# Cross attention with a maxout layer on one core: the first batch's casts and products in another order and on other engines

## The chip, the cores and the metric

The kernel runs on one core of one Trainium2 chip. A core has five engines with a queue each, which work their instructions off in order and wait for one another by semaphores: TensorE (PE in the profile; PEld is its loading of weights), VectorE (DVE), ScalarE (ACT), GpSimd (POOL) and SyncE (SP), which here issues nearly all transfers. The metric is the device time in microseconds (us) of one execution; it is compared by the median of several.

## The reference

There are 8 batches of 8 heads. In each, 512 rows of `x` attend to 32 rows of `state` and the other way round, with 64 elements per row. Both results, joined, are the input of a layer with two weights and a maximum, and an output weight.

```python
a = softmax(scale * x @ state.T);   xread = a @ state       # per batch and head
a2 = softmax(scale * state @ x.T);  sread = a2 @ x
t = concatenate([xread, sread])     # rows of all heads: (4352, 512)
h1 = t @ w1; h2 = t @ w2            # 512 x 1024 each
out = maximum(h1, h2) @ w_out       # 1024 x 512, result in float32
```

## The kernel before

**Algebra.** max(h1, h2) is relu(h1 − h2) + h2. So the kernel forms WD = W1 − W2 (`wd`) and W2Wo = W2 @ Wo (`wwo`), and since xread is a @ state it also forms state @ WD and state @ W2Wo per batch (the tiles `sw`, functions `sw_mm` and `sw_ev`). Per batch, the first layer is then relu(a · (state·WD)) (`l1_mm`, `l1_ev`, tile `r`), and the output is r @ Wo + a · (state·W2Wo) (`l2_part`, `l2_open`, tile `acc`). All matmuls are in bfloat16; the inputs arrive in float32 and are cast.

**Stages.** From batch 2 on the work is a steady loop. Batch 0, and the preparation of the weights beside it, is written out call by call in lines 604 to 877, and the order of these lines is the order on every engine's queue (a manual schedule; waits are added where data or a buffer require them). The change lies there, in lines 668 to 745.

**Loads.** SP's queue loads `x` of batch 0, then the first quarter (256 columns) of W2, W1 and Wo in two halves of 128 columns, then the other three quarters, then batches 1 to 3. W1, W2 and Wo have three float32 buffers each (`w1f`, `w2f`, `wof`), so the fourth quarter of W2 (line 623) waits until the first quarter's buffer has been read for the last time, which is the subtraction `w_sub(0, ...)`.

**Attention of batch 0.** Heads go in four pairs, k = 0 to 3. For each pair the exponentials `e` are summed over 32 states, the sums of two pairs are inverted together (`norm_sums`), and `e` is multiplied by the inverses into `a`: for pairs 0 and 1 together by `norm_mul(0, 0, "P")` on GpSimd (128x512 elements), for pair 3 by `norm_mul_pair` on VectorE (128x256), and for pair 2 in two halves of 128 elements, one on GpSimd and one on VectorE. `at_mm` transposes `a` on TensorE and `at_ev` copies it out of PSUM (tile `aT`); `l1_mm` needs both copies.

**Weights of the first quarter**, by halves j of 128 columns: `w2_cast_h`, `w1_cast_h`, `wo_cast_h` cast them; `sw_h_mm(j)` forms state·W1 − state·W2 from the casts, without waiting for `wd`; `w2_tr_h_mm` and `w2_tr_h_ev` transpose W2; `w_wo_h_mm(i, j)` is one W2Wo matmul for row block i and half j, `w_wo_ev(0, i)` copies the sum of both halves into the float32 tile `w2acc`. Later quarters do it with `w2_cast`, `w_sub`, `w2_tr_mm`, `w_wo_mm(r, i)` and `sw_two_mm`.

**PSUM** has two pools of four banks, `ps` and `pa`; a call's pool argument chooses. The tiles `acc` of batch 0 hold four banks of `pa` from `l2_part` on. **`idle(n)`** issues n matmuls of a zero tile with 256 columns, which compute nothing that is used.

An engine is named by a letter in the calls: "P" GpSimd, "V" VectorE, "A" ScalarE. All copies and casts go through one helper, so their lines in the profile are 58 (ScalarE), 60 (VectorE) and 62 (GpSimd).

Of the kernel before, what the change touches and what calls it, by code (L numbers as in the profile page):

```python
# [15 lines left out]
def kernel(  # L16
# [11 lines left out]
    _, _, Ns, _ = state.shape  # L28
# [3 lines left out]
    NC = S // 128  # L32
# [14 lines left out]
    pa = ctx.enter_context(tc.tile_pool(name="pa", bufs=4, space=bass.MemoryType.PSUM))  # L47
    ctx.enter_context(tc.manual_schedule())

    def bank(dtype=F32, pool=None):  # L50
        n = 512 if dtype == F32 else 1024
        if pool is pa:
            return pa.tile([128, n], dtype, tag="acc", name="acc")
        return ps.tile([128, n], dtype, tag="ps", name="ps")

    def copy(eng, o, i):
        if eng == "A":
            nc.scalar.copy(o, i)  # L58
        elif eng == "V":
            nc.vector.tensor_copy(o, i)  # L60
        else:
            nc.gpsimd.tensor_copy(o, i)  # L62
# [74 lines left out]
    P = {}  # L137
# [5 lines left out]
    def state_mm(b, pool=None):  # L143
        p = P["st", b] = bank(BF16, pool)
        nc.tensor.transpose(p[:, 0:128], sb0[:, b], ident)
# [69 lines left out]
    def xt_pair_ev(b, k, eng):  # L215
        copy(eng, st[b]["xt"][:, :, k, :], P["xt", k][:, 0:512].rearrange("p (c t) -> p c t", c=NC))
# [79 lines left out]
    def norm_sums(b, hh, sums=True):  # L296
        d = st[b]
        if sums:
            ev = d["e"].rearrange("p g c i n -> p (g c) i n")[:, :, 2 * hh:2 * hh + 2, :]
            nc.vector.tensor_reduce(d["es"][:, hh], ev, axis=mybir.AxisListType.X, op=ALU.add)  # L300
        nc.vector.reciprocal(d["er"][:, hh], d["es"][:, hh])

    def norm_mul(b, hh, eng):
        d = st[b]
        ev = d["e"].rearrange("p g c i n -> p (g c) i n")[:, :, 2 * hh:2 * hh + 2, :]
        av = d["a"].rearrange("p g c i n -> p (g c) i n")[:, :, 2 * hh:2 * hh + 2, :]
        (nc.gpsimd if eng == "P" else nc.vector).tensor_mul(  # L307
            av, ev, d["er"][:, hh].unsqueeze(3).to_broadcast([128, 2 * NC, 2, Ns]))

    def norm_mul_pair(b, k, eng, g0=0, g1=2):  # L310
        d = st[b]
        gs = slice(NC * g0, NC * g1)
        ev = d["e"].rearrange("p g c i n -> p (g c) i n")[:, gs, k, :]
        av = d["a"].rearrange("p g c i n -> p (g c) i n")[:, gs, k, :]
        (nc.gpsimd if eng == "P" else nc.vector).tensor_mul(
            av, ev, d["er"][:, k // 2, gs, k % 2].unsqueeze(2).to_broadcast([128, NC * (g1 - g0), Ns]))

    def norm(b, hh, eng, sums=True):
        norm_sums(b, hh, sums)
# [13 lines left out]
    def at_mm(b, g, pool=None):  # L333
        if b not in AT:
            AT[b] = keep.tile([128, 2, NC, 128], BF16, tag="at", name="aT")
        p = P["at", g] = bank(BF16, pool)
        for c in range(NC):
            nc.tensor.transpose(p[:, c * 128:(c + 1) * 128], st[b]["a"][:, g, c].rearrange("p i n -> p (i n)"), ident)

    def at_ev(b, g, eng):  # L340
        copy(eng, AT[b][:, g].rearrange("p c t -> p (c t)"), P["at", g][:, 0:512])
# [12 lines left out]
    def sread_norm(b):  # L354
        d = st[b]
        sr = d["sr"] = at.tile([128, 2, D], BF16, tag="sr", name="sr")
        rr = at.tile([128, 2], F32, tag="rr", name="rr")
        pv = d["srp"][:, 0:130].rearrange("p (g d) -> p g d", g=2)
        for g in range(2):
            nc.vector.reciprocal(rr[:, g:g + 1], pv[:, g, 64 * g:64 * g + 1])  # L360
        for g in range(2):
            nc.vector.tensor_scalar(sr[:, g, :], pv[:, g, 1 - g:65 - g], scalar1=rr[:, g:g + 1], scalar2=None,
                                    op0=ALU.mult)
# [21 lines left out]
    def sw_ev(b, lo, hi, g, eng):  # L385
        copy(eng, SW[b][:, g, lo:hi], P["sw", b, lo][g][:, 0:hi - lo])
# [28 lines left out]
    def sw_h_mm(j, pool):  # L415

        cs = slice(128 * j, 128 * j + 128)
        pg = P["sw", 0, 128 * j] = [bank(F32, pool), bank(F32, pool)]
        for t, w in ((sbd[:, 0], w1b), (sbdn, w2b[0])):
            for i in range(4):  # L420
                for g in range(2):
                    nc.tensor.matmul(pg[g][32 * i:32 * i + 32, 0:128], t[64 * g:64 * g + 64, i, 32 * g:32 * g + 32],
                                     w[64 * g:64 * g + 64, i, cs], start=(w is w1b), stop=(w is not w1b))
# [18 lines left out]
    def l1_mm(b, f, pool=None):  # L442
        if b not in R:
            R[b] = big.tile([128, NF, NC * 128], BF16, tag="r", name="r")
        p = P["l1", f] = bank(F32, pool)
        for g in range(2):
            nc.tensor.matmul(p, SW[b][:, g, f * 128:(f + 1) * 128], AT[b][:, g].rearrange("p c t -> p (c t)"),  # L447
                             start=(g == 0), stop=(g == 1))
# [71 lines left out]
    def w2_cast(q, eng):  # L520
        w2b[q] = stage.tile([128, 4, FQ], BF16, tag="w2b", bufs=2, name="w2b")
        for j, e in enumerate(eng):
            m = 4 // len(eng)
            copy(e, w2b[q][:, m * j:m * j + m].rearrange("p i f -> p (i f)"),
                 w2f[q][:, m * j:m * j + m].rearrange("p i f -> p (i f)"))

    def w2_cast_h(j, eng):
        if 0 not in w2b:
            w2b[0] = stage.tile([128, 4, FQ], BF16, tag="w2b", bufs=2, name="w2b")
        copy(eng, w2b[0][:, :, 128 * j:128 * j + 128], w2f[0][:, :, 128 * j:128 * j + 128])  # L530

    def w1_cast_h(j, eng):
        copy(eng, w1b[:, :, 128 * j:128 * j + 128], w1f[0][:, :, 128 * j:128 * j + 128])

    def wo_cast_h(j, eng):
        copy(eng, wo[:, j, :], wof[0][:, j, :])

    def w2_tr_h_mm(j, pool=None):
        p = P["w2h", j] = bank(BF16, pool)
        for i in range(4):  # L540
            nc.tensor.transpose(p[:, i * 128:(i + 1) * 128], w2b[0][:, i, j * 128:(j + 1) * 128], ident)

    def w2_tr_h_ev(j, eng):
        copy(eng, w2t[:, j].rearrange("p i t -> p (i t)"), P["w2h", j][:, 0:512])
# [15 lines left out]
    def w_sub(q, i0, i1, eng):  # L560
        (nc.gpsimd if eng == "P" else nc.vector).tensor_sub(  # L561
            wd[:, i0:i1, q * FQ:(q + 1) * FQ], w1f[q][:, i0:i1], w2f[q][:, i0:i1])
# [15 lines left out]
    def w_wo_h_mm(i, j, pool=None):  # L578
        if j == 0:
            P["wwo", 0, i] = bank(F32, pool)  # L580
        nc.tensor.matmul(P["wwo", 0, i], w2t[:, j, i, :], wo[:, j, :], start=(j == 0), stop=(j == 1))

    def w_wo_ev(r, i, eng):
        if r == 0:
            copy(eng, w2acc[:, i, :], P["wwo", r, i])
        else:
            nc.vector.tensor_tensor(wwo[:, i, :] if r == len(ROUNDS) - 1 else w2acc[:, i, :], P["wwo", r, i],  # L587
                                    w2acc[:, i, :], op=ALU.add)
# [3 lines left out]
    def idle(n, cols=256):  # L592
        if idle_p[0] is None:
            idle_p[0] = bank(F32, pa)
        for j in range(n):
            nc.tensor.matmul(idle_p[0][:, 0:cols], wz[:, 0:128], wz[:, 0:cols], start=True, stop=True)  # L596
# [71 lines left out]
    xt_pair_mm(0, 3)  # L668
    norm_sums(0, 0, False)
    norm_mul(0, 0, "P")  # L670
    xt_pair_ev(0, 3, "A")
    idle(1)
    scores_pair_mm(0, 2, None)
# [10 lines left out]
    sw_h_mm(0, pa)  # L684
    reduce_pair(0, 3)
    norm_sums(0, 1, False)
    norm_mul_pair(0, 2, "P", 0, 1)
    norm_mul_pair(0, 3, "V")
    norm_mul_pair(0, 2, "V", 1, 2)
    wo_cast_h(0, "P")  # L690
    w1_cast_h(1, "P")
    w2_tr_h_ev(0, "A")
    sw_ev(0, 0, 128, 1, "A")
    idle(4)
    at_mm(0, 0)
    sw_ev(0, 0, 128, 0, "A")
    at_mm(0, 1)
    w_wo_h_mm(1, 0, pa)
    wo_cast_h(1, "P")
    w_sub(0, 0, 4, "P")  # L700
    w_wo_h_mm(3, 0)
    w2_cast_h(1, "A")
    at_ev(0, 1, "V")
    sw_h_mm(1, pa)
    sw_ev(0, 128, 256, 1, "V")
    w2_tr_h_mm(1)
    at_ev(0, 0, "A")
    l1_mm(0, 0)
    sw_ev(0, 128, 256, 0, "A")
    l1_mm(0, 1, pa)  # L710
    w_wo_h_mm(0, 0, pa)
    w2_tr_h_ev(1, "A")
    l1_ev(0, 1, "A")
    copy("A", sb0[:, 1], sf0[:, 1])
# [1 line left out]
    l1_ev(0, 0, "V")  # L716
    w_wo_h_mm(3, 1)
    w_wo_ev(0, 3, "A")
    w2_cast(1, "P")
    w_wo_h_mm(0, 1)  # L720
    w_wo_h_mm(1, 1)
    w_wo_h_mm(2, 1)
    state_mm(1)
    sread_norm(0)
    state_ev(1, "V")
    l2_part(0, 3)
    sw_mm(1, 0, FQ)
    w_wo_ev(0, 1, "A")
    sw_ev(1, 0, FQ, 1, "A")
    l2_part(0, 1)  # L730
    sw_ev(1, 0, FQ, 0, "A")
# [6 lines left out]
    wo_cast_part(1, 1, "P")  # L738
    sw_two_mm(1)
    sw_two_ev(1, 1, "V")  # L740
    w_wo_ev(0, 0, "A")
    l2_part(0, 2)
    w_wo_mm(1, 1)
    w_wo_ev(1, 1, "V")
    w_wo_ev(0, 2, "A")
    w_wo_mm(1, 2)
    sw_two_ev(1, 0, "A")
    l1_mm(0, 3)
# [131 lines left out]
    for b in range(1, B):  # L880
        n = b + 1
# [68 lines left out]
```

## Time and profile before

| | |
|---|---|
| median of 6 executions | 147.06 us (146.8 to 147.61) |
| the profiled execution | 147.61 us, span on the core 145.8 us |
| TensorE busy | 139.2 us, 95% of the span |
| VectorE, ScalarE, GpSimd busy | 85.4, 70.3, 59.4 us |
| transfers | 29.44 MB, 202 GB/s on average, 320 to 364 GB/s from 3.6 to 33 us |

In a row of the timeline the first number is the start in us from the beginning of the span, the second how long the operation or the merged group took; then come engine, line, operation, what it writes and reads, shape and count, and in brackets the engine's idle time before it with what ended it. A row of the chain has start, length and what the time went to. Rows of merged instructions overlap a little, as the next one starts while the last is ending.

### The profile page before, as it was taken

How to read it: one execution, taken by the hardware profiler on the slowest of the kernel's cores; microseconds unless marked ns; L12 is line 12 of the kernel's file. 1: busy time of each engine (PE TensorE's matmuls, PEld its weight loads, DVE VectorE, ACT ScalarE, POOL GpSimd, SP SyncE). 2: the span in 40 equal slices, each digit the busy share in tenths (PEclk: the TensorE clock that was granted, in tenths of full speed). 3: DMA queues.
4: the chain of work that ended last, by engine and by line, in shares of the span. 5: the costliest groups of instructions: out<-in, count | busy, mean ns of one | idle time of the engine just before them, and what ended most of it. 6: DMA issues, size and time to landing. Idle time of an engine off the chain costs nothing.

```text
span 145.8 us, 3202 instructions
## 1 busy us (share of the span) xinstructions
PE 139.2 (95%) x1281; PEld 69.8 (48%) x1300; DVE 85.4 (59%) x176; ACT 70.3 (48%) x136; POOL 59.4 (41%) x82
## 2 busy tenths in 40 slices
PE   6899999999999999999999999999999999999990
PEld 4465444464554445444544544454445344754460
DVE  3595776879788648464854675376557464621110
ACT  4478757786694456326450825271537145511010
POOL 2379633858938431925290547226500500000000
PEclk9999999999999999999999999999999999999999
DMA  5999999999979999388948784887406032402423
GB/s 119 322 321 349 356 362 364 361 349 201 108 153 357 149 321 274 74 195 329 246 52 280 288 180 86 278 295 141 72 18 272 7 72 108 180 4 72 144 101 115
DMA packets 37727, 29.44 MB, mean 202 GB/s; under 512 B 21328, under 2 KB 34896, under 8 KB 36816
## 3 DMA queue, kind: packets, MB, share of 16 engines
q1 hardware_dynamic: 37440, 29.17, 71.4%
q8 instruction: 10, 0.16, 0.5%
q10 hardware_dynamic: 272, 0.07, 0.2%
q14 instruction: 5, 0.04, 0.1%
HBM read 15.34 MB, written 8.91 MB: 166 GB/s over the span
## 4 chain that ended last, share of the span: by engine, by line
PE 77%; DMA 9%; SPq 6%; POOL 3%; DVE 2%; issue 1%; ACT 0%; POOLq 0%
PE acc L463 35%; PE ps L447 16%; PE acc L459 7%; DMA wof<-in_moe_w_out_dram 5%; DMA xt<-xb 4%; PE ps L576 3%; PE ps L503 2%; PE acc L513 2%; PE ps L382 2%; PE ps L284 2%; SPq L130 2%; PE acc L349 1%; SPq L134 1%; SPq L91 1%; PE acc L487 1%
## 5 line engine op out<-in xcount | busy, mean ns | idle before, releaser
L463 PE MATMUL acc<-wo,r 128*128 128x512 bf16 x246 | 59.3, 379 | 0.4
L463 PEld LDWEIGHTS <-r 128*128 128x128 bf16 x248 | 23.8, 98 | 28.7 <-issue 0.6
L58 ACT COPY ob<-acc 128x512 f32<-128x512 f32 (+2 forms) x17 | 9.4, 554 | 48.1 <-PE acc L463 26.7
L447 PE MATMUL ps<-aT,sw 128*128 128x512 bf16 x117 | 27.7, 379 | 0.0
L438 DVE TENSOR_SCALAR r<-ps 128x512 bf16<-128x512 f32 x26 | 18.0, 691 | 14.3 <-PE ps L447 14.2
L307 POOL TENSOR_TENSOR a<-e,er 128x512 bf16<-128x512 bf16 x14 | 14.4, 1049 | 25.8 <-ACT e L289 18.9
L436 ACT ACTIVATE r<-ps 128x512 bf16<-128x512 f32 x33 | 19.6, 602 | 5.5 <-PE ps L447 4.9
L60 DVE COPY ob<-acc 128x512 f32<-128x512 f32 (+1 forms) x17 | 10.9, 646 | 16.3 <-PE acc L463 14.6
L62 POOL CAST xb<-xf 128x1024 bf16<-128x1024 f32 x12 | 12.9, 1082 | 16.4 <-DMA xf<-in_x_dram 16.4
L62 POOL CAST xo<-xf 128x512 bf16<-128x512 f32 x28 | 16.4, 623 | 5.8 <-DMA xf<-in_x_dram 5.4
L447 PEld LDWEIGHTS <-sw 128*128 128x128 bf16 x128 | 12.2, 98 | 13.7
L459 PE MATMUL acc<-sw,aT 128*128 128x512 bf16 x49 | 15.5, 381 | 0.3
L60 DVE CAST sw<-ps 128x512 bf16<-128x512 f32 x15 | 9.8, 686 | 9.9 <-PE ps L382 9.5
L58 ACT CAST sw<-ps 128x512 bf16<-128x512 f32 (+1 forms) x21 | 11.0, 573 | 3.0 <-PE ps L408 1.5
L300 DVE TENSOR_REDUCE es<-e 128x16 f32<-128x512 bf16 x14 | 9.2, 656 | 1.7 <-ACT e L289 1.7
L289 ACT ACTIVATE e<-ps 128x512 bf16<-128x512 f32 x14 | 7.7, 596 | 0.8 <-PE ps L284 0.2
L596 PE MATMUL acc<-wz 128*128 128x256 bf16 x32 | 6.7, 345 | 1.2 <-DVE ones L636 1.2
L459 PEld LDWEIGHTS <-aT 128*128 128x128 bf16 x62 | 5.0, 98 | 4.4
L576 PE MATMUL ps<-wo,w2t 128*128 128x512 bf16 x23 | 6.6, 379 | 0.2
L587 DVE TENSOR_TENSOR w2acc<-ps,w2acc 128x512 f32<-128x512 f32 x8 | 5.1, 684 | 1.2 <-PE ps L576 1.2
L561 POOL TENSOR_TENSOR wd<-w1f,w2f 128x1024 bf16<-128x1024 f32 x2 | 4.7, 2365 | 1.7 <-DMA w1f<-in_moe_w_dram 1.7
L284 PEld LDWEIGHTS <-xt 128*128 128x128 bf16 x112 | 4.3, 98 | 1.9 <-DMA xt<-xb 0.2
(109 smaller groups left out, 146.4 us busy)
## 6 DMA issues: line engine op xcount, KB each, us to landing
xf<-in_x_dram SPq DMA_DIRECT2D x14, 512.0 KB, 5.6
out_dram<-ob SPq DMA_DIRECT2D x7, 1024.0 KB, 4.2
w2f<-in_moe_w_dram SPq DMA_DIRECT2D x3, 512.0 KB, 7.4
xf<-in_x_dram SPq DMA_DIRECT2D x4, 256.0 KB, 3.9
w1f<-in_moe_w_dram SPq DMA_DIRECT2D x4, 256.0 KB, 6.6
wof<-in_moe_w_out_dram SPq DMA_DIRECT2D x4, 256.0 KB, 6.8
w1f<-in_moe_w_dram SPq DMA_DIRECT2D x2, 512.0 KB, 9.0
wof<-in_moe_w_out_dram SPq DMA_DIRECT2D x2, 512.0 KB, 8.8
```

What stands on the lines that cost most here:

```text
L58: nc.scalar.copy(o, i)
L60: nc.vector.tensor_copy(o, i)
L62: nc.gpsimd.tensor_copy(o, i)
L289: nc.scalar.activation(out=ev.rearrange("p (g c) i n -> p g c (i n)", g=2), in_=P["sc", hh].rearrange("p (c g m) -> p g c m", c=NC, g=2), ...
L300: nc.vector.tensor_reduce(d["es"][:, hh], ev, axis=mybir.AxisListType.X, op=ALU.add)
L307: (nc.gpsimd if eng == "P" else nc.vector).tensor_mul(av, ev, d["er"][:, hh].unsqueeze(3).to_broadcast([128, 2 * NC, 2, Ns]))
L436: nc.scalar.activation(out=o, in_=p, func=ACTF.Relu)
L438: nc.vector.tensor_scalar(o, p, scalar1=0.0, scalar2=None, op0=ALU.max)
L447: nc.tensor.matmul(p, SW[b][:, g, f * 128:(f + 1) * 128], AT[b][:, g].rearrange("p c t -> p (c t)"), start=(g == 0), stop=(g == 1))
L459: nc.tensor.matmul(p, AT[b][:, g, c, :], SW[b][:, g, FF:WC], start=(start and g == 0), stop=(stop and g == 1))
L463: nc.tensor.matmul(p, R[b][:, f, c * 128:(c + 1) * 128], wo[:, f, :], start=(start and j == 0), stop=(stop and j == len(fs) - 1))
L576: nc.tensor.matmul(p, w2t[:, f, i, :], wo[:, f, :], start=(f == fs[0]), stop=(f == fs[-1]))
```

## The change

The quarter product of pair 2 leaves GpSimd, and the whole of pair 2 is multiplied by VectorE ahead of pair 3. GpSimd casts half 0 of Wo and half 1 of W1 directly behind its first product. The four idle matmuls ahead of `at_mm` go, and two W2Wo matmuls, which stood behind `at_mm`, take their place. Half 1 of W2 is cast by VectorE and no longer by ScalarE, ahead of `at_ev(0, 1)`. The first quarter's subtraction is issued in two halves, one ahead of the cast of Wo's half 1 and one behind it, and the cast of W2's second quarter follows directly. Three of the copies into `w2acc` are issued earlier on ScalarE, and some tiles change their PSUM pool.

```diff
-    def norm_mul_pair(b, k, eng, g0=0, g1=2):
+    def norm_mul_pair(b, k, eng):
...
     norm_mul(0, 0, "P")
+    wo_cast_h(0, "P")
+    w1_cast_h(1, "P")
     xt_pair_ev(0, 3, "A")
...
     norm_sums(0, 1, False)
-    norm_mul_pair(0, 2, "P", 0, 1)
+    norm_mul_pair(0, 2, "V")
     norm_mul_pair(0, 3, "V")
-    norm_mul_pair(0, 2, "V", 1, 2)
-    wo_cast_h(0, "P")
-    w1_cast_h(1, "P")
     w2_tr_h_ev(0, "A")
     sw_ev(0, 0, 128, 1, "A")
-    idle(4)
+    sw_ev(0, 0, 128, 0, "A")
+    w_wo_h_mm(1, 0, pa)
+    w_wo_h_mm(3, 0, pa)
     at_mm(0, 0)
-    sw_ev(0, 0, 128, 0, "A")
     at_mm(0, 1)
-    w_wo_h_mm(1, 0, pa)
+    w2_cast_h(1, "V")
+    w_sub(0, 0, 2, "P")
     wo_cast_h(1, "P")
-    w_sub(0, 0, 4, "P")
-    w_wo_h_mm(3, 0)
-    w2_cast_h(1, "A")
+    w_sub(0, 2, 4, "P")
+    w2_cast(1, "P")
     at_ev(0, 1, "V")
-    sw_h_mm(1, pa)
+    at_ev(0, 0, "A")
+    sw_h_mm(1, None)
     sw_ev(0, 128, 256, 1, "V")
-    w2_tr_h_mm(1)
-    at_ev(0, 0, "A")
+    w2_tr_h_mm(1, pa)
     l1_mm(0, 0)
     sw_ev(0, 128, 256, 0, "A")
-    l1_mm(0, 1, pa)
-    w_wo_h_mm(0, 0, pa)
+    l1_mm(0, 1)
+    w_wo_h_mm(0, 0)
...
     w_wo_ev(0, 3, "A")
-    w2_cast(1, "P")
     w_wo_h_mm(0, 1)
     w_wo_h_mm(1, 1)
+    w_wo_ev(0, 1, "A")
+    w_wo_ev(0, 0, "A")
     w_wo_h_mm(2, 1)
+    w_wo_ev(0, 2, "A")
     state_mm(1)
...
     sw_mm(1, 0, FQ)
-    w_wo_ev(0, 1, "A")
     sw_ev(1, 0, FQ, 1, "A")
...
-    w_wo_ev(0, 0, "A")
     l2_part(0, 2)
...
-    w_wo_ev(0, 2, "A")
     w_wo_mm(1, 2)
```

More of the change, by code (lines that the diff above doesn't have):

```diff
@@ L308, in norm_mul @@
             av, ev, d["er"][:, hh].unsqueeze(3).to_broadcast([128, 2 * NC, 2, Ns]))
-    def norm_mul_pair(b, k, eng, g0=0, g1=2):
+    def norm_mul_pair(b, k, eng):
         d = st[b]
-        gs = slice(NC * g0, NC * g1)
-        ev = d["e"].rearrange("p g c i n -> p (g c) i n")[:, gs, k, :]
-        av = d["a"].rearrange("p g c i n -> p (g c) i n")[:, gs, k, :]
+        ev = d["e"].rearrange("p g c i n -> p (g c) i n")[:, :, k, :]
+        av = d["a"].rearrange("p g c i n -> p (g c) i n")[:, :, k, :]
         (nc.gpsimd if eng == "P" else nc.vector).tensor_mul(
-            av, ev, d["er"][:, k // 2, gs, k % 2].unsqueeze(2).to_broadcast([128, NC * (g1 - g0), Ns]))
+            av, ev, d["er"][:, k // 2, :, k % 2].unsqueeze(2).to_broadcast([128, 2 * NC, Ns]))
     def norm(b, hh, eng, sums=True):
```

## The prediction

> **What bounds the kernel now.** I read first the page's shares and its chain of work that ended last, then that chain in order of time for the first 20 us, because the whole change lies between 8.9 and 17 us.
>
> ```profile
> PE 139.2 (95%) x1281; PEld 69.8 (48%) x1300; DVE 85.4 (59%) x176; ACT 70.3 (48%) x136; POOL 59.4 (41%) x82
> ...
> PE 77%; DMA 9%; SPq 6%; POOL 3%; DVE 2%; issue 1%; ACT 0%; POOLq 0%
> ```
> ```profile
> 9.84 7.41 DMA wof<-in_moe_w_out_dram
> 17.25 0.05 issue
> 17.30 0.61 POOL wo L62
> ...
> 17.99 0.62 POOL wo L62
> 18.62 0.04 issue
> 18.66 0.81 PE ps L576 x3
> ```
>
> From 18.66 us on the chain is TensorE almost without a break. Before that it is the Wo transfer of the second quarter (issued 9.84, landed 17.25; its second half landed 17.94), cast by GpSimd until 18.61, and w_wo_mm(1,1)'s second matmul at 18.66. So TensorE's order in the changed stage has slack: its matmuls start at 18.21 and 18.66 where their usual distance is 0.21, a wait of 0.24 us, and sw_two_mm(1) (17.20 to 17.77, against 0.34 for the same work at 22.55) stands 0.23 us for VectorE's subtraction that ends at 17.38, itself late by its DMA (landed 16.00 and 16.57). A third wait, 0.10 us at 20.70, is for the W2 cast that ends at 20.65. **About 0.57 us of delay is swallowed, and a gain is swallowed whole**, since the transfers land 1.36 to 1.50 us apart per 512 KB from 19.46 to 28.16 whatever their issue times.
>
> Next VectorE's and GpSimd's rows in order of time, for operations that overlap.
>
> ```profile
> 34.94 0.88 DVE L307 TENSOR_TENSOR a<-e,er 128x512 bf16<-128x512 bf16 x1
> ...
> 39.58 0.72 DVE L60 COPY sbd<-stt 64x128 bf16<-64x128 bf16 x1
> ```
> ```profile
> 6.78 0.95 POOL L156 TENSOR_SCALAR sbdn<-sbd 128x256 bf16<-128x256 bf16 x1
> ...
> 34.22 1.05 POOL L307 TENSOR_TENSOR a<-e,er 128x512 bf16<-128x512 bf16 x1 [0.60 <-DVE er L301]
> 35.21 1.50 POOL L62 CAST xb<-xf 128x1024 bf16<-128x1024 f32 x1
> ...
> 39.16 2.06 POOL L62 CAST xb<-xf 128x1024 bf16<-128x1024 f32 x2
> ```
> ```profile
> 10.10 0.83 DVE L315 TENSOR_TENSOR a<-e,er 128x256 bf16<-128x256 bf16 x2
> ```
> ```profile
> 10.21 0.58 POOL L315 TENSOR_TENSOR a<-e,er 128x128 bf16<-128x128 bf16 x1 [0.26 <-DVE er L301]
> 10.73 0.67 POOL L62 CAST wo<-wof 128x512 bf16<-128x512 f32 x1
> ```
>
> **They take turns.** VectorE's product of 34.94 ends at 35.82, 0.55 us after GpSimd's ended at 35.27; the cast behind it took 1.50 instead of 1.04 and ended 0.89 after 35.82. VectorE's copy at 39.58 of only 128 elements took 0.72: it ended 0.11 after the cast that ended at 40.20. At 10.1 it goes three times: VectorE's 128x256 product to 10.53, GpSimd's quarter 0.26 after it (10.79), VectorE's 128x128 0.14 after that (10.93), the Wo cast 0.46 after that (11.39). So a product on VectorE and any of these on GpSimd exclude each other, and each one waiting gets the next turn. Prices after a wait: product 0.28 for 128x256 (half of 0.55), GpSimd's cast of 128x512 0.46.
>
> **The change, part by part.** The sum is made against the profiled execution: 147.61 us with a span of 145.8, so 1.8 outside it; it is the slowest of the six, whose median is 147.06, and I add the difference to the median.
>
> *TensorE's own work:* idle(4) goes (10.42 to 10.87 in the rows: 0.45 us). w_wo_h_mm(1,0) and (3,0), 0.21 us each, go ahead of at_mm. They lie before the slack: worth nothing by themselves.
>
> *GpSimd's order.* Today after its first product (ends 9.95): quarter product, Wo half 0 (to 11.39), W1 half 1 (to 11.95), Wo half 1 (12.10 to 12.71), subtraction (12.68 to 15.04), W2 cast (14.99 to 16.03). Then: Wo half 0 needs only its landing, 3.83 + 5.7 = 9.5; it starts at 9.90 and ends 0.56 (the distance of casts in a row) after 9.95, at 10.51. VectorE's 128x256 product for pair 2 starts at 10.10 as today [...]: 10.51 + 0.28 = 10.79. W1 half 1 (landed 4.38 + 6.0 = 10.4) has its turn: 10.79 + 0.46 = 11.25. VectorE's pair 3: 11.25 + 0.28 = **11.53, against 10.93 today** for the last product. Both casts could lie between only because the quarter that GpSimd had waited for the same reciprocal.
>
> *W2's second half* lands at 11.31 (ScalarE's cast starts at 11.33 on it) and now two wait for it: GpSimd's first half of the subtraction and, behind pair 3, VectorE's cast. GpSimd's starts follow a landing by 0.05 to 0.15 us, so it asks at 11.36 to 11.46, before 11.53, and has the turn: 2.36/2 = 1.18, less 0.05 of start: 12.67.
>
> *VectorE's cast of W2:* 0.43 us alone (three casts xo<-xf of this shape, 427 ns), about 0.28 after a wait. Whether it waits at all is the open point. [...] The copy at 39.58 agrees; but the one f32 cast beside GpSimd work, at 7.05, took its usual 0.43 while the 0.95 us operation of 6.78 ran to 7.73. That operation may itself have waited (it ended 0.25 after the cast), so the row doesn't decide. By the rule W2 is ready at 12.67 + 0.28 = **12.95**, by the row at 11.83; ScalarE has it at 11.95 today. I take the rule, as the copy at 39.58 is nearest in kind; the other end is the rival below.
>
> *Who waits behind it:* on VectorE at_ev(0,1), +0.34: 13.29. On TensorE the second half of sw_h_mm(1) from 13.0, W2's transposes, then l1_mm(0,0), which needs that eviction: 13.40 instead of 12.48, **+0.92**. ScalarE is relieved of its 0.62 cast (at_ev(0,0) ends near 12.6) but that isn't last. Wo half 1 comes behind the cast: 12.95 + 0.46 = 13.41, needed at 14.69: hidden. The second half of the subtraction ends near 14.6, the W2 cast near 15.6, needed at 17.5: hidden; today's covers were 15.04 and 16.03.
>
> *ScalarE's four w2acc evictions in a row* and the banks: in today's program each new PSUM tile takes the bank released longest ago. By that rule sw_mm(1)'s second bank is the one of w_wo(0,0), whose eviction is now third. They follow each other by 0.48 (14.22, 14.70 today); the first can start at 14.22 + 0.92 = 15.14 and the third ends near 16.7. The states' copies, what sw_mm(1) waits for today (15.56), would allow 16.48; so it starts at 16.72: **+1.16**. If the banks fall otherwise, +0.92 remains.
>
> *The sum:* 1.16 − 0.23 − 0.24 + 0.09 (VectorE's W2 transposes eviction now late, so the 18.66 matmul starts behind it) = 0.78 at w_wo_mm(1,2); −0.10 at 20.70 = **+0.68**. After that TensorE has no wait of 0.1 us until 41.9, and there the chain (scores, products, casts, transposing DMA) shifts with it. 145.8 + 0.68 = 146.5 span; 147.61 + 0.68 = 148.3 for such an execution; 147.06 + 0.68 = **147.7** as median. Without the bank wait 0.43; with two starts later than I think 0.9: own range 147.4 to 148.0.
>
> *DMA queue:* SP's load of W2's fourth quarter waits for the subtraction (SP's waits: 2.5 us, issued 15.07); it goes out some 0.4 us earlier. Landings are spaced by the stream (20.94, 22.44, 23.81), so 0.
>
> **The rivals.**
> *Swallowed (not slower):* one race, at 11.53. If GpSimd asks more than 0.06 us after VectorE lets go (11.59), or casts don't exclude it, VectorE's cast is done at 11.83, l1_mm(0,0) starts at 12.72 (at_mm ends late: aT at 12.67), +0.24; the third eviction then gives sw_mm(1) +0.47, under the 0.57 of slack: 147.06. For it: GpSimd's margin is 0.07 to 0.17 us and the row at 7.05. Against: four alternations in the rows.
> *Faster:* the earlier issue of W2's fourth quarter or the freer ScalarE reaches past 18.66. It would need TensorE waits there; they sum to 0.1 up to 27 us. 146.6 at best.
> *The clock:* [...] Row first: the 15 idle matmuls at 1.19 took 3.38 us (0.225 each), those at 10.42 0.11 each; the page's PEclk digits are 9 in both, so they don't tell. In my timeline TensorE stands at most 0.9 us at once (12.1 to 13.0)[...].
>
> **How the numbers follow.** Turns lost, +0.4 to +0.9: 0.52. Swallowed: 0.32. Clock or further waits: 0.10. Faster: 0.06. 0.3% (0.44 us) is about what a measurement of this kernel tells from no change. Slower: most of the first (0.46), the third, a little of the second: 0.58. Same: 0.36. Faster: 0.06. Range 146.8 to 148.3: from the swallowed case's scatter to the first case's upper end and part of the third.
>
> **What would show it.** Right: VectorE's two 128x256 products end near 10.8 and 11.5; its W2 cast is shown with over 1 us; l1_mm(0,0) starts near 13.4, the third w2acc eviction ends just before sw_mm(1); w_wo_mm(1,2) comes 0.8 us later than 18.87. Wrong: the W2 cast ends before 12, or w_wo_mm(1,2) stays at 18.87; or matmuls of 128x512 stand 0.43 apart (the clock).

## The result and the profile after

The changed kernel takes 148.22 us (median of 34 executions), the kernel before 147.45 us (median of 71 taken beside it and before). The ratio is 1.0049, with a 95% interval of 1.0033 to 1.0065: **slower by 0.72 us**, where 0.64 us over the median of then (147.06) was forecast. Ratios here leave out executions more than 1.5% above the fastest of their kernel, in e3 two of six and the profiled one among them.

The profiled execution of the changed kernel took 148.36 us with a span of 146.6. From its page, the engines' shares and the chain that ended last:

```profile
PE 138.3 (94%) x1277; PEld 69.3 (47%) x1296; DVE 87.8 (60%) x177; ACT 69.7 (48%) x135; POOL 60.3 (41%) x82
...
PE 88%; DMA 4%; DVE 3%; issue 1%; SPq 1%; ACT 1%
```

TensorE works 0.9 us less (the four idle matmuls, 0.45 us, are part of it) and yet the end comes later. VectorE has joined the chain. In order of time the chain shows where, in the stage of the change:

```profile
10.51 1.43 DVE a L314 x2
11.94 1.42 DVE w2b L60
13.36 0.04 issue
13.40 0.25 PE ps L421 x8
```

Before, this place in the chain was a transfer (Wo's second quarter, 9.84 to 17.25). Now it is VectorE's two products and its W2 cast. TensorE's waits from 8 to 45 us say the same, in us in total, times and the longest:

```profile
PE ps L213 <- DVE xo L60: 0.7, 1, 0.7
PE ps L421 <- DVE w2b L60: 0.6, 1, 0.6
PE ps L337 <- DVE a L314: 0.3, 1, 0.3
```

The first is the last piece of `x`, which landed 0.41 us later in this execution (7.44) than in the profiled one of before (7.03); all of the stage starts later by that. The other two are new. Now VectorE's rows and then GpSimd's, in order of time, of the changed kernel:

```profile
10.51 1.43 DVE L314 TENSOR_TENSOR a<-e,er 128x256 bf16<-128x256 bf16 x2
11.86 1.49 DVE L60 CAST w2b<-w2f 128x512 bf16<-128x512 f32 x1
13.27 0.41 DVE L60 COPY aT<-ps 128x512 bf16<-128x512 bf16 x1
```
```profile
10.30 0.61 POOL L62 CAST wo<-wof 128x512 bf16<-128x512 f32 x1
10.85 0.81 POOL L62 CAST w1b<-w1f 128x512 bf16<-128x512 f32 x1
11.63 1.44 POOL L560 TENSOR_TENSOR wd<-w1f,w2f 128x512 bf16<-128x512 f32 x1
13.02 0.80 POOL L62 CAST wo<-wof 128x512 bf16<-128x512 f32 x1
```

The two engines take turns throughout: Wo cast to 10.91, first product to 11.19, W1 cast to 11.66, second product to 11.94, half of the subtraction to 13.07, W2 cast to 13.35. Each is longer than alone by its wait: the W2 cast 1.49 instead of 0.43, the W1 cast 0.81 instead of 0.61. l1_mm(0,0) starts at 13.82, 6.38 after the landing of `x`; before it was 12.48, 5.45 after it.

### The profile page after: what moved, and what is told of

Same layout as the page of the kernel before. It is cut to its first block, busy times and chain, and to the rows that moved or that the text cites. A ratio compares the mean times of both kernels' runs of the same rounds, so it can differ in the third digit from the quotient of the medians.

```text
span 146.6 us, 3192 instructions
## 1 busy us (share of the span) xinstructions
PE 138.3 (94%) x1277; PEld 69.3 (47%) x1296; DVE 87.8 (60%) x177; ACT 69.7 (48%) x135; POOL 60.3 (41%) x82
## 4 chain that ended last, share of the span: by engine, by line
PE 88%; DMA 4%; DVE 3%; issue 1%; SPq 1%; ACT 1%
PE acc L462 37%; PE ps L446 17%; PE acc L458 8%; DMA xf<-in_x_dram 4%; PE ps L575 3%; PE ps L381 3%; PE ps L502 2%; PE acc L512 2%; PE ps L284 2%; PE acc L348 1%; PE acc L486 1%; PE acc L446 1%; PE acc L510 1%; DVE a L314 1%; DVE w2b L60 1%
## 5 line engine op out<-in xcount | busy, mean ns | idle before, releaser
L435 ACT ACTIVATE r<-ps 128x512 bf16<-128x512 f32 x34 | 20.3, 601 | 6.8 <-PE ps L446 6.3
L60 DVE CAST sw<-ps 128x512 bf16<-128x512 f32 (+1 forms) x16 | 10.1, 661 | 9.8 <-PE ps L381 9.4
L58 ACT CAST sw<-ps 128x512 bf16<-128x512 f32 (+2 forms) x22 | 11.4, 564 | 3.9 <-PE ps L407 2.3
L595 PE MATMUL acc<-wz 128*128 128x256 bf16 x28 | 5.7, 343 | 1.2 <-DVE ones L635 1.2
L62 POOL CAST w2b<-w2f 128x1024 bf16<-128x1024 f32 (+1 forms) x4 | 4.4, 1098 | 3.4 <-DMA w2f<-in_moe_w_dram 3.4
L560 POOL TENSOR_TENSOR wd<-w1f,w2f 128x512 bf16<-128x512 f32 (+1 forms) x3 | 5.1, 1685 | 1.1 <-DMA w1f<-in_moe_w_dram 1.1
```

What stands on the lines that cost most here:

```text
L435: nc.scalar.activation(out=o, in_=p, func=ACTF.Relu)
```

## The experiments

Landings move by about a microsecond from execution to execution (VectorE's first product, which follows them, starts at 9.73 us in e4b and at 10.81 in e6), so the starts of one profile are not compared directly with those of another. The table takes three differences within each profiled execution (us): the end of VectorE's last product minus the landing of W2's half 1; l1_mm(0,0) minus the landing of the last piece of `x`; and l1_mm(0,3), with which TensorE leaves the stage, minus the landing of Wo's second quarter. The ratio is to the kernel before.

| kernel | W2 cast takes | product − W2 | l1_mm(0,0) − x | l1_mm(0,3) − Wo | ratio (95%) |
|---|---|---|---|---|---|
| before | 0.62 (ScalarE) | −0.37 | 5.45 | 1.36 | 1 |
| changed | 1.49 | 0.39 | 6.38 | 3.22 | 1.0049 (1.0033 to 1.0065) |
| a1, changed again | 1.49 | 0.40 | 6.56 | 1.98 | |
| a2, changed again | 1.49 | 0.39 | 6.53 | 2.21 | |
| e1, subtraction behind | 0.42 | 0.36 | 5.74 | 1.37 | 0.9986 (0.9950 to 1.0023) |
| e2, W2 on ScalarE | 0.62 | 0.48 | 5.82 | 1.51 | 1.0005 (0.9977 to 1.0033) |
| e3, whole subtraction ahead | 2.57 | 0.36 | 7.62 | 3.86 | 1.0154 (1.0073 to 1.0235) |
| e4, idle back | 0.41 | 0.11 | 5.82 | 1.90 | 1.0033 (1.0006 to 1.0060) |
| e4b, the same | 0.43 | 0.06 | 6.10 | 1.44 | |
| e4c, the same | 1.49 | 0.40 | 6.46 | 2.21 | |
| e5, W1 on ScalarE | 0.43 | −0.07 | 5.53 | 1.37 | 0.9981 (0.9956 to 1.0005) |
| e8, the same again | 0.43 | 0.06 | 5.38 | 1.36 | 1.0012 (0.9979 to 1.0045) |
| e6, no collision | 0.43 | 0.01 | 5.40 | 1.36 | 0.9993 (0.9964 to 1.0022) |
| e7, VectorE's W2 cast in the kernel before | 0.83 | 0.41 | 6.50 | 3.32 | 1.0008 (0.9985 to 1.0032) |

**e1: the subtraction whole behind the Wo cast.** Against the changed kernel:

```diff
     w2_cast_h(1, "V")
-    w_sub(0, 0, 2, "P")
     wo_cast_h(1, "P")
-    w_sub(0, 2, 4, "P")
+    w_sub(0, 0, 4, "P")
```

> The changed kernel, but GpSimd's subtraction stands whole behind the cast of Wo's half 1, so GpSimd waits for that landing (12.05 us in the profile before) while VectorE casts W2's half 1. [...] the W2 cast takes 0.43 us instead of 1.49, l1_mm(0,0) starts about 1.1 us earlier than in the changed kernel relative to the end of the last product, and the time goes back to that of before: ratio 1.000, within 0.997 to 1.003. Rival, TensorE's order (two W2Wo matmuls in place of idle ones) or ScalarE's four copies in a row: unchanged from the change, ratio 1.005.

Measured: 147.45 us, beside 147.56 for the kernel before. VectorE's rows of e1:

```profile
10.19 1.44 DVE L314 TENSOR_TENSOR a<-e,er 128x256 bf16<-128x256 bf16 x2
11.55 0.41 DVE L60 CAST w2b<-w2f 128x512 bf16<-128x512 f32 x1
```

The products still take 1.44 us together, so the first collisions stand. The W2 cast takes its plain time, and no loss can be told: it hangs on the one turn of the cast against the subtraction. l1_mm(0,0) starts 1.13 us after the last product, where the changed kernel has 1.88: 0.75 us earlier and not 1.1, as the transposes (to 12.30) and the copy to `aT` (to 12.76) lie between in any case. TensorE's order, without the idle matmuls, and ScalarE's four copies in a row are all still in e1 and cost nothing there that can be told.

**e2: ScalarE casts W2's half 1**, GpSimd as in the change:

```diff
-    w2_cast_h(1, "V")
+    w2_cast_h(1, "A")
```

> The changed kernel, but ScalarE casts W2's half 1 again, as before; GpSimd's order is that of the change. [...] the cast takes 0.62 us from its landing whatever GpSimd does, VectorE's aT copy is no longer held, l1_mm(0,0) is about 0.2 us later than before instead of 0.9: ratio 1.000, within 0.997 to 1.003; the two products still take 1.43 us together. Rival, the products' delay alone is what costs: ratio stays near 1.005.

Measured: ratio 1.0005, with l1_mm(0,0) 0.37 us later than before (0.2 expected). The subtraction ahead of the Wo cast costs nothing that can be told when nobody stands behind it. This and e1 undo the loss from its two sides.

**e3: the whole subtraction ahead**, so that what the cast waits for is doubled:

```diff
     w2_cast_h(1, "V")
-    w_sub(0, 0, 2, "P")
+    w_sub(0, 0, 4, "P")
     wo_cast_h(1, "P")
-    w_sub(0, 2, 4, "P")
```

> The changed kernel, but the whole subtraction (2.36 us instead of a half of 1.18) stands ahead of the cast of Wo's half 1, so what VectorE's W2 cast stands behind is doubled. [...] the W2 cast takes about 2.7 us instead of 1.49, l1_mm(0,0) starts 1.2 us later still, and as the slack is used up all of it reaches the end: about 1.15 us over the changed kernel, ratio 1.013. Rival, the W2 cast's wait is hidden or something else sets l1_mm: ratio 1.005.

Measured: ratio 1.0154, l1_mm(0,0) 1.06 to 1.24 us later than in the three profiles of the change. The six executions lie at 148.41, 149.33 and four times 150.6 to 150.8, where 1.013 would be 149.4; the profiled one is of the last four and shows what puts it above that. For the other three the same cause is likely and not shown. VectorE's rows of e3, and after them GpSimd's:

```profile
11.90 2.56 DVE L60 CAST w2b<-w2f 128x512 bf16<-128x512 f32 x1
...
25.43 2.59 DVE L60 CAST wo<-wof 128x1024 bf16<-128x1024 f32 x1
```
```profile
11.69 2.50 POOL L560 TENSOR_TENSOR wd<-w1f,w2f 128x1024 bf16<-128x1024 f32 x1
...
24.98 2.35 POOL L560 TENSOR_TENSOR wd<-w1f,w2f 128x1024 bf16<-128x1024 f32 x1 [1.75 <-DMA w1f<-in_moe_w_dram]
```

The first pair is the dose: the cast is held for the whole subtraction. The second pair is new: VectorE is by now so late that its Wo cast of the third quarter (0.69 us at 23.84 in the kernel before) comes behind the last quarter's subtraction. TensorE's waits of e3 give it 1.3 us:

```profile
PE ps L421 <- DVE w2b L60: 1.7, 1, 1.7
PE ps L575 <- DVE wo L60: 1.3, 1, 1.3
```

**e4: the four idle matmuls back**, ahead of A's transposes:

```diff
     w_wo_h_mm(3, 0, pa)
+    idle(4)
     at_mm(0, 0)
```

> The changed kernel with the four idle matmuls (0.45 us) back, ahead of A's transposes. [...] TensorE waits 0.5 to 0.7 us there for the last product, so they fit into the wait: ratio 1.005, as the change, with l1_mm(0,0) where it was. Rival, the clock[...]: matmuls behind it faster and ratio 1.000. Rival, TensorE's own order is the path there: 0.3 to 0.4 us later, ratio 1.008.

Measured: 1.0033, an interval that overlaps that of the change (1.0033 to 1.0065) and tells the two apart neither way. The profile of it, VectorE's rows and GpSimd's, had the turn fall the other way:

```profile
9.89 1.44 DVE L314 TENSOR_TENSOR a<-e,er 128x256 bf16<-128x256 bf16 x2
11.26 0.41 DVE L60 CAST w2b<-w2f 128x512 bf16<-128x512 f32 x1
```
```profile
11.29 1.51 POOL L560 TENSOR_TENSOR wd<-w1f,w2f 128x512 bf16<-128x512 f32 x1 [0.23 <-DMA w2f<-in_moe_w_dram]
```

Here the last product ended at 11.33, 0.11 after W2's landing. GpSimd's row starts 0.04 before that end, VectorE has the turn nevertheless, and GpSimd's subtraction is the one that is longer (1.51 instead of 1.26). Further executions of the changed kernel and of e4 tell more.

> The changed kernel itself, another execution. [...] who casts or subtracts first on W2's half 1 is settled by whether GpSimd has begun the subtraction well before VectorE's last product ends. Where that product ends 0.3 us or more after W2's landing, the W2 cast takes about 1.5 us and l1_mm(0,0) starts some 1.9 us after the last product; where it ends 0.1 us after, the cast takes 0.43 and l1_mm(0,0) starts 1.3 us after it. Rival, a fixed order: the cast takes 1.5 us in every execution.

> As the one before it: a further execution of the changed kernel, for the distance of the last product's end from W2's landing, and the length of the W2 cast that goes with it (1.5 us or 0.43 us).

> The changed kernel with the four idle matmuls back, a further execution, as the first one had the turn fall to VectorE. [...] with the last product ending 0.3 us or more after W2's landing the W2 cast takes 1.5 us, and l1_mm(0,0) starts 6.4 to 6.6 us after the last landing of x, as without the idle matmuls. Rival, TensorE's order: 0.3 to 0.4 us later than that.

> The same once more: l1_mm(0,0) 6.4 to 6.6 us after the last landing of x where GpSimd has the turn, about 5.8 where VectorE has it.

All three profiles of the changed kernel have the product end 0.39 or 0.40 after W2's landing, and the cast at 1.49. Of the three of e4 one has 0.40 and 1.49, two have 0.06 and 0.11 and a plain cast. Who has the turn goes with that distance, and the distance moves with the landings. VectorE's rows of e4c and GpSimd's beside them, the case that was lost:

```profile
10.24 1.44 DVE L314 TENSOR_TENSOR a<-e,er 128x256 bf16<-128x256 bf16 x2
11.60 1.49 DVE L60 CAST w2b<-w2f 128x512 bf16<-128x512 f32 x1
```
```profile
11.37 1.43 POOL L560 TENSOR_TENSOR wd<-w1f,w2f 128x512 bf16<-128x512 f32 x1
```

In it l1_mm(0,0) stands at 6.46, within the 6.38 to 6.56 of the three profiles without idle matmuls: where the turn is lost, the 0.45 us of idle work fits into the wait. Whether the idle matmuls shift how often it is lost, three profiles can't tell.

**e5 and e8: W1's half 1 cast by ScalarE**, so that nothing of GpSimd's comes between the two products:

```diff
     norm_mul(0, 0, "P")
     wo_cast_h(0, "P")
-    w1_cast_h(1, "P")
...
     sw_ev(0, 0, 128, 0, "A")
+    w1_cast_h(1, "A")
     w_wo_h_mm(1, 0, pa)
```

> The changed kernel with W1's half 1 cast by ScalarE, so that GpSimd's cast no longer comes between VectorE's two products. [...] the products take about 0.95 us together instead of 1.43 (the first still waits for the Wo cast), end before W2's half 1 lands, VectorE then answers the landing first (0.02 us against 0.05 to 0.15 for GpSimd), the W2 cast takes about 0.43 us and the ratio is 1.000. If GpSimd has the turn all the same, the cast takes 1.5 us and the ratio stays at 1.003 to 1.005.

> The changed kernel with W1's half 1 cast by ScalarE, measured again, as its first interval (0.9956 to 1.0005) leaves a small gain open. Theory of the swallowed gain: ratio 1.000, interval across 1. Rival, the earlier first layer is worth something at the end: ratio 0.998 again, both intervals together below 1.

Measured: 0.9981 and 1.0012, both intervals across 1, so no gain that can be told. VectorE's rows of e5 and then GpSimd's:

```profile
9.85 1.17 DVE L314 TENSOR_TENSOR a<-e,er 128x256 bf16<-128x256 bf16 x2
11.12 0.43 DVE L60 CAST w2b<-w2f 128x512 bf16<-128x512 f32 x1
```
```profile
11.22 1.46 POOL L560 TENSOR_TENSOR wd<-w1f,w2f 128x512 bf16<-128x512 f32 x1 [0.81 <-issue]
```

The second product ends before W2 lands, VectorE answers the landing 0.10 us before GpSimd's row starts, and no loss can be told though subtraction and cast stand where the change put them. So the W1 cast between the products counts only by letting the next turn be lost. The products took 1.17 us where 0.95 was expected: the wait for the Wo cast (9.81 to 10.42 in the same execution) was in that sum, but the cast ended 0.57 us after the first product had started, in the changed kernel 0.40.

**e6: neither collision**, e5 and e1 together.

> The same with the subtraction whole behind the cast of Wo's half 1, so that neither collision is left. l1_mm(0,0) then starts some 0.3 us earlier than in the kernel before, relative to the last landing of x. Theory of the swallowed gain: the Wo transfer's landing sets the second matmul of w_wo_mm(1,1) all the same, ratio 1.000, within 0.997 to 1.003. Rival, the front of the stage counts in full: ratio 0.998.

Measured: 0.9993. l1_mm(0,0) is as early as in the kernel before (5.40 against 5.45; I had expected 0.3 us earlier). e8's is 5.38.

**e7: one part of the change alone**, in the kernel before:

```diff
-    w2_cast_h(1, "A")
+    w2_cast_h(1, "V")
```

> The kernel before with one part of the change alone: W2's half 1 cast by VectorE. VectorE is idle at its landing (its last product ended 0.4 us earlier) and GpSimd's casts are short. [...] the cast takes 0.43 to 0.6 us, GpSimd's W1 cast of 11.34 may wait 0.3 us for it, l1_mm(0,0) within 0.3 us of before: ratio 1.000, within 0.997 to 1.003. Rival, VectorE is the wrong engine for this cast whatever stands beside it: ratio 1.003 or more.

Measured: 1.0008, no difference. The profiled execution is not a usual one (148.41 us, the clock, below); in it the cast took 0.83, as it had to wait for GpSimd's cast of Wo. Behind casts of 0.6 us the loss of a turn is small (0.83 instead of 0.43); the half subtraction of 1.2 us makes it matter.

## Why the prediction was right

**The turns: right, with their prices.** Moved by the 0.41 us that `x` landed later, the steps were forecast for 11.20 (first product), 11.94 (second), 13.08 (half subtraction), 13.36 (W2 cast), 13.70 (the aT copy) and 13.81 (l1_mm(0,0)); the profile has 11.19, 11.94, 13.07, 13.35, 13.68 and 13.82. The price after a wait held too: W1's cast ended 0.47 after the product (0.46 forecast). By the row of 7.05 an f32 cast might have gone through beside GpSimd's work (0.43 us, beside an operation of 0.95). W2's cast doesn't: it took 1.49 us against 0.43 and ended 0.28 after the half subtraction (13.35 and 13.07), and in e3 0.27 after the whole one (14.46 and 14.19). That a cast, too, is held up until the other's operation has ended was my estimate, by the copy at 39.58, and for this cast it was right; what sets it apart from the one at 7.05 is not shown. e1, e2 and e3 take the cause away from two sides and double it, and the time follows.

**The bank wait: wrong.** The step "by that rule sw_mm(1)'s second bank is the one of w_wo(0,0)" failed. The third copy into w2acc ended at 17.13, and sw_mm(1)'s last seven matmuls had started from 16.89 on, 0.05 after the states' copy: +0.92 at sw_mm(1) (16.89 minus 15.56, less 0.41) instead of +1.16. ScalarE's third copy and those matmuls, in the changed kernel:

```profile
16.52 0.61 ACT L58 COPY w2acc<-ps 128x512 f32<-128x512 f32 x1
16.89 0.30 PE L381 MATMUL ps<-wd,sbd 64*32 64x256 bf16 x7
```

The same shows in every profile: sw_mm(1) follows l1_mm(0,0) by 3.07 or 3.08 us, in the kernel before as well. Which bank it takes, and in what order banks are taken again, the profile does not name.

**The slack: right for the execution that it was read from, but not a constant.** The sum let 0.38 us be swallowed up to w_wo_mm(1,2) and l1_mm(0,3) behind it (0.23 + 0.24 − 0.09). In 13 of the 14 profiles l1_mm(0,3) starts, to within 0.02 us, at the later of two points: 6.45 us after l1_mm(0,0), or 1.36 us after the Wo landing. The first and last of these layers, in the kernel before and in a1:

```profile
12.48 0.59 PE L447 MATMUL ps<-aT,sw 128*128 128x512 bf16 x2
19.30 1.02 PE L447 MATMUL ps<-aT,sw 128*128 128x512 bf16 x4
```
```profile
13.39 0.81 PE L446 MATMUL ps<-aT,sw 128*128 128x512 bf16 x3
19.84 1.03 PE L446 MATMUL ps<-aT,sw 128*128 128x512 bf16 x4
```

They are 6.82 and 6.45 apart, so the slack before was 0.37 us, as forecast. But it is set by how late Wo lands after `x`: 10.91 us in that execution, 9.63 to 11.11 in the fourteen. With l1_mm(0,0) at 5.45 as before, the slack would be 0 in five of them, 0.57 at most, and 0.23 on average (an estimate from these distances). So with the turn lost l1_mm(0,3) stands 1.98, 2.21 and 2.21 behind the Wo landing (a1, a2, e4c) instead of 1.36, which is 0.62 to 0.85 too late. In the first profile of the change the Wo landing came early (17.19), so that its 3.22 isn't a price. That profile is also the one of the 14 that fits neither point (6.60 after l1_mm(0,0)): VectorE's subtraction for the second quarter loses turns to GpSimd's Wo casts there and takes 1.85 instead of 1.29. Whether that is the reason is not shown, as it loses one in a2 and e4c too and l1_mm(0,3) keeps its 6.45.

**The total: partly luck.** With the turn lost, l1_mm(0,0) was 0.93 to 1.11 us late (6.38 to 6.56, less 5.45), 1.03 on average of four, where 0.92 was forecast. Less 0.23 of average slack, and less the 0.10 at 20.70 (w2_tr_mm(2) follows l1_mm(0,3) by 1.29 or 1.30 in a1, a2 and e4c, before by 1.40), that makes an estimated 0.70, beside 0.72 measured. The forecast's 0.68 had 0.24 too much for the bank and about as much too little in the other two terms.

**The rivals.** "Swallowed" is a real outcome of the same order of instructions on VectorE and GpSimd: two of e4's three profiles are it, though none of the three of the changed kernel, and the sum's margin, GpSimd asking before the last product ends, was the right point; what was forecast at 0.32 for a whole kernel happens in single executions. The clock: 128x512 matmuls of the changed kernel stand 0.21 to 0.22 us apart from 13.82 on. The mean granted clock lies below 0.99 in 8 of the 34 executions of the changed kernel and in 31 of the 136 of the kernel before that were taken beside the experiments, about a quarter of both; among the others the medians are 147.9 and 147.3, so the loss is there without it. "Faster": SP's wait for the subtraction fell from 2.5 to 1.7 us, and the transfers behind it land 1.36 to 1.51 us apart as before, so nothing came of it; e8 keeps that order with the front as early as before, and shows no gain.

## What to carry to other kernels

Before work is moved between VectorE and GpSimd, list what the other of the two runs at that moment. Here VectorE's products of 128x256 and its cast of W2 waited until a GpSimd cast or subtraction had ended, and GpSimd's next cast then waited for them (0.81 us instead of 0.61). So a cast of 0.43 us on the path took 0.83 beside a GpSimd cast of 0.67 (e7), 1.49 beside the half subtraction of 1.44 (the change) and 2.56 beside the whole one of 2.50 (e3). When two engines wait for the same landing, the order of their turns can hang on a few tenths of a microsecond (here 0.11 against 0.39 us from landing to free engine) and change from execution to execution: make the long one wait for something later, as e1 does. And measure slack as the distance between the events that can decide (here l1_mm(0,0) plus 6.45 us and the Wo landing plus 1.36), in more than one execution, since it moves with the landings.

## What the runs showed of the hardware that was not expected

- **A turn seems to be asked for later than the row's start.** GpSimd's subtraction started 0.04 us before VectorE's product ended (e4) and lost; starting 0.29 (e3) or 0.31 before (the change, e4c) it won. I had estimated 0.05 to 0.15 for start and asking together, from the landing on; between 0.04 and 0.29 the runs show nothing.
- **Half the clock after a short wait.** In the profiled execution of e7 TensorE waited 1.23 us for GpSimd's cast of a piece of `x` that landed late, and then worked at half rate for 3.4 us. TensorE's row after that wait, and then two stretches of e7 with TensorE's busy time, the granted clock, the busy share of the DMA engines and GB/s:

```profile
7.54 0.54 PE L213 MATMUL ps<-ident,xo 128*128 128x128 bf16 x4 [1.23 <-POOL xo L62]
```
```profile
4.25:7.66 3.41, 1.75 (x23) 1.00 0.99 301
7.66:11.07 3.41, 3.41 (x28) 0.50 1.14 326
```

An idle matmul of 256 columns takes 0.42 at 7.87, where it took 0.27 at 7.77 in the kernel before, and those of 9.03 stand 0.21 apart instead of 0.11 (three at 9.75 in the kernel before). In the 3.41 us ahead of the drop TensorE was busy for 1.75 us. In the changed kernel it was busy for 1.84 us of a stretch of that length (4.70 to 8.11), and the granted clock of the next one (8.11 to 11.52) was 1.00. Where the limit lies, and whether it is one of busy time, no run here shows. So a longest stand of 0.9 us, as the prediction has it, was too weak a reason to rule the clock out. The half rate is likely, not shown, to be part of why that execution took 148.41 us, 0.9 above the median of e7. Its mean granted clock was 0.988; executions of the kernel before with one as low (31 of 136, above) have a median of 148.6 us, the others 147.3. None of those was profiled.
